# A recurrent attention kernel: the first chunk's float32 score products of a pair's two halves issued alternately

## The chip, the cores and the metric

The kernel runs on one core of one Trainium2 chip. The metric is the device time of one execution in microseconds (us). A kernel's time is the median of several runs. The profile and the trace come from one execution that was recorded by the hardware profiler.

## What is computed

The input is r, k, v, w, a, b of 4 batches x 8 heads x 768 steps x 40 elements, and the weights of two feed-forward layers. For each of the 32 heads a 40x40 state is carried over the 768 steps; then two layers work on all 3072 tokens. Cut to what matters:

```python
for t in range(S):                       # S = 768
    y[:, :, t] = einsum('bhd,bhde->bhe', r_t, state)
    Sa = einsum('bhde,bhe->bhd', state, a_t)
    state = state * w_t[:, :, None, :] - einsum('bhd,bhe->bhde', Sa, b_t)
    state = state + einsum('bhd,bhe->bhde', v_t, k_t)
x = y as 3072 tokens x 320
h = x @ w_in;  x = (h * cos(h)) @ w_out              # 320 -> 2048 -> 320
h = x @ w_in2; x = (s * relu(h)**2 + b) @ w_out2     # 320 -> 2048 -> 320
```

## The kernel before, in words

The 768 steps are cut into 12 chunks of 64 steps (`C = 64`), and the recurrence is solved chunk by chunk with matrix products. The 32 heads are 4 groups `g` of 8 (`l` counts the 8). Two groups are a pair `pg`, and they are the pair's two halves: the first lies on partitions 0 to 39, the second on partitions 64 to 103 of the same tiles.

`prep(c)` (line 1117) makes what a chunk needs of its own inputs. `load_w` brings the decays into `XX`, `scan` multiplies them up on VectorE, `stage_kb` and `stage_ar` scale k, b and a, r by them, `tz` transposes, and `sc1` (line 733) makes the first score products: for each of the 8 heads of a group one product of k and b (128 columns) with a (64 columns) over the 40 elements of a head, into one PSUM bank `s1p`. VectorE multiplies the bank with a mask and writes `M1`, and ScalarE copies the diagonal blocks of it to `ND`. When all four groups have done so, `inv_begin`, `inv`, `inv_out`, `inv_mid` and `inv_end` (lines 757 to 806) invert the triangular blocks: a transpose of `ND` to `UN`, then 30 small VectorE instructions in a row that read each other's results (`ND<-UD,UN` and `UD<-ND,UD` by turns), and products on TensorE that end in `DT`.

`chain(c, pg)` (line 1140) solves one pair of a chunk: `rhs`, `u_half`, `lmul`, `u_half` find the updates `UF` (`uhp` and `rhp` are their PSUM tiles), `sp` carries the state on, `tx` (line 902; `tx0`, line 913, in the first chunk) transposes `UF` into `XT` with a ScalarE copy behind it, `sc2` (line 924) makes the second score products of `XT` (128 columns) with r (64 columns) into a bank `s2p`, VectorE masks that into `M2`, and `yt` multiplies into the output `y`. `xs` writes y to DRAM (`x<-yhl`), and `x1_load` reads it back as the input of the first layer (`xs<-x`). `mlp` then issues the two layers in steps: `hp` is the PSUM tile of the first product and `op` that of the second; the tile `q` between them lies in a ring of 8 buffers that it shares with `XT`, `M2`, `y` and `o1`.

In chunks 1 to 11 the scores are taken from float16 parts that are stacked on 120 partitions. In the first chunk (c = 0) `sc1` and `sc2` work on float32 directly, on the 40 partitions of one half, in groups of 8 products of the same half:

```python
r = slice(g % 2 * 64, g % 2 * 64 + 40)
...
nc.tensor.matmul(ps[:, l, :], k, a, start=(l == 0), stop=True, skip_group_check=True)
```

A float32 product stands in the trace as two weight loads and two matmul records, so a group's 8 products are 16 records.

The order of the instructions on the engines isn't the order of these calls. Each call of `do` (line 1113) is a block, and every engine instruction of it is only recorded (class `Recorder`, from line 95). `schedule` (line 275) then plans all of them in one list: each instruction (for TensorE the run of products in a block) has a cost from `cost` (line 151) and a priority, which is the longest way from it to the end by these costs; whichever can start first is emitted next, and the engines run the emitted order without change. `cost` tells how long a weight load and a matmul are held to take, and it halves both where a product has at most 64 columns of weights (`side`, line 161). A block may only start when its tiles have buffers, and `caps` (line 1168) limits how many tiles of a name may be alive: `XT` 2, `M2` 2, `q` 4, and 6 of the 8 PSUM banks for all that isn't `hp` or `op` (`att`). The limit is looked at when a block starts; `tx0` takes two `XT` tiles in one block.

Since all instructions are recorded, they are emitted by line 392, and the trace has that line for nearly all of them. They are told apart by the names of their tiles.

Of the kernel before, what the change touches and what calls it, by code (L numbers as in the profile page):

```python
# [24 lines left out]
C = 64  # L25
# [69 lines left out]
class Recorder:  # L95
# [54 lines left out]
    @staticmethod  # L150
    def cost(eng, method, out, ins, k):
        size = lambda x: math.prod(c for _, c in list(x.ap)[1:])
        n = size(out)
        psum = any(x.space == PSUM for x in ins)
        if eng == "tensor":

            k, m, f = ins[0].ap[0][1], size(ins[0]), 1 + (ins[0].dtype == F32)
            if method == "transpose":
                return k * f, m * f, k / 128, k * f * f
            low = Recorder.region(out)[0] < 64  # L160
            n, side = size(ins[1]) * f * f, 2 if m <= 64 else 1
            return n if low else 0, (32 if m == 128 and f == 1 else m * f * f) / side, k / 128, n / side
        if eng == "scalar":
            return (0.05 if psum else 0.092) + n * 0.833e-3 + (0.093 if k.get("accum_out") is not None else 0) + \
                (0.093 if isinstance(k.get("bias"), bass.AP) else 0)
        if eng == "vector":
            if method == "reciprocal":
                return 0.065 + n * 6.3e-3
            if method == "tensor_tensor_scan":
                return 0.065 + n * 2.08e-3  # L170
            if method == "transpose":
                return 0.065 + n * 1.87e-3
            if method == "tensor_reduce":
                return 0.065 + size(ins[0]) * 1.04e-3
            half = method in ("tensor_scalar", "tensor_copy", "memset") and not (psum and ins[0].dtype == F32)
            return 0.065 + n * (0.52e-3 if half else 1.04e-3) + (0.063 if isinstance(k.get("scalar"), bass.AP) else 0)
        if eng == "gpsimd":
            if method in ("tensor_scalar", "memset"):
                return 0.05 + n * (1.03e-3 if method == "tensor_scalar" else 0.8e-3)
            return 0.147 + n * (2.1e-3 if out.dtype == F32 else 1.887e-3)  # L180
        b = WIDTH.get(out.dtype, 4) * math.prod(c for _, c in out.ap)
        run = min(Recorder.run(x) for x in (out, *ins) if x.ap[-1][0] == 1)
        full = max(x.ap[0][1] for x in (out, *ins) if x.space != DRAM) == 128
        return 0.45 if full else 0.625, b / (360e3 if run >= 512 else 180e3)
# [247 lines left out]
class Fast:  # L432
# [300 lines left out]
    def sc1(self, c, g):  # L733
        nc = self.nc
        ps = self.pp.tile([128, 8, C], F32, tag="at", bufs=8, name="s1p")
        for l in range(8):
            if c == 0:
                r = slice(g % 2 * 64, g % 2 * 64 + 40)
                k = self.IN["kb", c, g // 2][r, l].rearrange("p m t -> p (m t)")
                a = self.A0[g // 2, 0][r, l]  # L740
            else:
                k, a = self.KB[c, g][0:120, l, :], self.AR[c, g][0:120, l, 0:C]
            nc.tensor.matmul(ps[:, l, :], k, a, start=(l == 0), stop=True, skip_group_check=True)
        if g == 0:
            self.ND[c] = self.pst.tile([128, 16, 32], F32, tag="ND", name="ND", bufs=1)
        m = self.M1[c, g] = self.pa.tile([128, 8, C], F32, tag="M1", name="M1", bufs=7)
# [177 lines left out]
    def sc2(self, c, g):  # L924
        nc = self.nc
        ps = self.pp.tile([128, 8, C], F32, tag="at", bufs=8, name="s2p")
        for l in range(8):
            if c == 0:
                r = slice(g % 2 * 64, g % 2 * 64 + 40)
                x, ar = self.XT[0, g, l // 4][r, l % 4, :], self.A0[g // 2, 1][r, l, :]  # L930
            else:
                x, ar = self.XT[c, g][0:120, l, :], self.AR[c, g][0:120, l, C:2 * C]
            nc.tensor.matmul(ps[:, l, :], x, ar, start=(l == 0), stop=True, skip_group_check=True)
        m = self.M2[c, g] = self.pm.tile([128, 8, C], F32, tag="q", name="M2", bufs=8)
        nc.vector.tensor_tensor(out=m, in0=ps, in1=bc(self.mask2, 1, [128, 8, C]), op=ALU.mult)

# [180 lines left out]
    def prep(self, c):  # L1117
# [4 lines left out]
        for pg in range(2):  # L1122
            do(self.load_stage, c, pg)
            do(self.stage_kb, c, pg)
            do(self.load_ar, c, pg)
            do(self.stage_ar, c, pg)
            do(self.kb_out, c, 2 * pg)
            do(self.kb_out, c, 2 * pg + 1)
            for g in (2 * pg, 2 * pg + 1):
                do(self.tz, c, g)  # L1130
                do(self.sc1, c, g)
        do(self.inv_begin, c)
        do(self.inv, c)
        do(self.inv_out, c)
# [4 lines left out]

    def chain(self, c, pg):  # L1140
        g0, g1 = 2 * pg, 2 * pg + 1
        for f in [(self.rhs, c, pg), (self.u_half, c, pg, 0), (self.lmul, c, pg), (self.u_half, c, pg, 1), (self.uhl, c, g0), (self.uhl, c, g1),
                  (self.sp, c, pg), (self.tx, c, g0), (self.sc2, c, g0), (self.tx, c, g1), (self.sc2, c, g1),
                  (self.yt, c, pg), (self.ts, c, pg)]:
            self.do(*f)

# [11 lines left out]
    def run(self, es0):  # L1158
# [3 lines left out]
        with ExitStack() as es:  # L1162
# [2 lines left out]
            self.x0 = dr.tile([NC, 2, 3, 40, 768], F16, name="x0")  # L1165
            self.x1 = dr.tile([NC, 2, 128, DM], F32, name="x1")
            self.consts(pc)
            rec = self.nc = Recorder(nc, {"any": {"at", "xs", "q"}, "cls": {"XT": 2, "rhp": 3, "hp": 2, "op": 2, "xs": 2, "M2": 2, "q": 4, "att": 6}})
            rec.sink.add(self.junk.tensor.name)
            pool = lambda s, n, **k: rec.pool(s.enter_context(tc.tile_pool(name=n, bufs=1, **k)), n)  # L1170
            self.pm = pool(es, "mlp")
# [205 lines left out]
```

## Time and profile before

| what | value |
|---|---|
| median of 3 runs | 1194.1 us (1187.11, 1194.1, 1196.09) |
| the profiled execution's own time | 1188.45 us |
| its span, first to last instruction | 1186.7 us |
| TensorE matmuls busy | 1024.5 us (86%), 16094 records |
| TensorE weight loads busy | 822.7 us (69%) |
| VectorE busy | 718.7 us (61%) |
| ScalarE busy | 740.1 us (62%) |
| GpSimd busy | 437.2 us (37%) |

The rows below use the profile's short names: PE is TensorE's matmuls, PEld its weight loads, DVE is VectorE, ACT is ScalarE, POOL is GpSimd and SP is the engine that issues the DMAs (SPq is its queue). A row of the timeline is: start in us, length in us, engine, line, operation, tiles out<-in, shapes, x the number of instructions that are merged in it, and in brackets the idle time before it with what ended it. A row of the chain of waits is: start, length, engine or DMA, tiles, line and count. A row of the windows is: the stretch, its length, then for PE, PEld, DVE, ACT and POOL the busy us and the count of instructions, the granted TensorE clock, the mean busy share of the DMA engines, and GB/s.

### The profile page before, as it was taken

What the parts mean: (1) busy time and instruction counts of PE and PEld (TensorE: products, weight loads), DVE (VectorE), ACT (ScalarE), POOL (GpSimd) and SP (SyncE); (2) the same over time, 40 slices, a digit from 0 to 9 for tenths busy, and PEclk for the clock granted to TensorE, in tenths of its full rate; (3) what the DMA queues carried; (4) which work ended last, traced back from release to release, by engine and by line L of the source; (5) the groups of instructions that cost most, each with busy time, mean ns of one, the idle gap of its engine ahead of it and who ended that gap; (6) DMA issues with size and microseconds to landing.
All of it is one profiled execution on the core that took longest, in us unless ns stands there. A gap on an engine that the chain in (4) does not pass through costs nothing.

```text
span 1186.7 us, 37912 instructions
## 1 busy us (share of the span) xinstructions
PE 1024.5 (86%) x16094; PEld 822.7 (69%) x16094; DVE 718.7 (61%) x1390; ACT 740.1 (62%) x1640; POOL 437.2 (37%) x430
## 2 busy tenths in 40 slices
PE   3335878988999889989989998976999999999996
PEld 3234767776778677767777776755788888888885
DVE  6989475857573849384846553789444455454543
ACT  4466568786767677677868674766544454444443
POOL 2685455465535464536454512358300000000000
PEclk9999969999999899989998899888999999999999
DMA  9553343444433543253443222475000000000001
GB/s 229 190 193 121 114 151 116 150 126 156 138 101 122 159 144 125 95 172 109 146 137 124 86 68 73 147 185 131 27 23 23 23 23 23 23 23 23 23 13 24
DMA packets 74755, 121.15 MB, mean 102 GB/s; under 512 B 16500, under 2 KB 47348, under 8 KB 73556
## 3 DMA queue, kind: packets, MB, share of 16 engines
q1 hardware_dynamic: 74580, 118.67, 33.1%
q8 instruction: 128, 2.10, 0.8%
q14 instruction: 47, 0.39, 0.1%
HBM read 72.71 MB, written 12.29 MB: 72 GB/s over the span
## 4 chain that ended last, share of the span: by engine, by line
PE 57%; DVE 13%; DMA 12%; ACT 7%; SPq 6%; issue 4%; POOL 0%; ACTq 0%; DVEq 0%; POOLq 0%
PE hp L392 23%; PE op L392 21%; SPq L392 6%; DMA XX<-in_w 4%; PE ytp L392 3%; PE rhp L392 3%; DVE XX L392 3%; DMA wraw<-in_w 3%; DVE wraw L392 2%; DMA XT<-XT 2%; PE uhp L392 2%; DVE v L392 1%; DMA xs<-x 1%; ACT XT L392 1%; DVE w L392 1%
## 5 line engine op out<-in xcount | busy, mean ns | idle before, releaser
L392 PEld LDWEIGHTS <-w 120*128 120x128 f16 (+1 forms) x3102 | 301.1, 100 | 98.8 <-ACT w L392 33.1
L392 PE MATMUL op<-v,gh 128*128 128x320 f16 x1536 | 328.5, 304 | 3.2 <-ACT gh L392 3.0
L392 PE MATMUL op<-v,gl 128*128 128x320 f16 x768 | 232.9, 303 | 2.6 <-POOL gl L392 2.6
L392 PE MATMUL hp<-xs,w 120*128 120x256 f16 x1536 | 208.8, 287 | 11.9 <-DMA xs<-x 10.7
L392 PE MATMUL hp<-x2s,w 120*128 120x256 f16 x1536 | 189.8, 272 | 0.0
L392 POOL TENSOR_TENSOR gl<-q,gh 128x512 f16<-128x512 f32 x96 | 116.9, 1220 | 197.0 <-ACT gh L392 191.8
L392 PEld LDWEIGHTS <-gh 128*128 128x128 f16 x1536 | 144.2, 99 | 52.2 <-ACT gh L392 3.6
L392 ACT ACTIVATE q<-hp 128x512 f32<-128x512 f32 x96 | 57.2, 596 | 126.3 <-PE hp L392 126.0
L392 DVE SCALAR_TENSOR_TENSOR q<-q,s_t 128x512 f32<-128x512 f32 x96 | 72.1, 751 | 102.6 <-ACT q L392 96.8
L392 DVE SCALAR_TENSOR_TENSOR q<-hp,q 128x512 f32<-128x512 f32 x96 | 65.3, 684 | 81.0 <-ACT q L392 78.3
L392 DVE SCALAR_TENSOR_TENSOR gl<-q,b_t,gh 128x512 f16<-128x512 f32 x96 | 72.1, 752 | 48.9 <-ACT gh L392 46.8
L392 PEld LDWEIGHTS <-gl 128*128 128x128 f16 x768 | 75.8, 99 | 35.2 <-POOL gl L392 3.8
L392 ACT ACTIVATE gh<-q,b_t 128x512 f16<-128x512 f32 x96 | 69.1, 720 | 42.9 <-DVE q L392 41.8
L392 DVE TENSOR_TENSOR_SCAN XX<-XX,starts 128x264 f32<-128x264 f32 x96 | 73.1, 816 | 29.2 <-DMA XX<-in_w 28.2
L392 ACT ACTIVATE q<-hp,half_pi 128x512 f32<-128x512 f32 x96 | 65.1, 681 | 36.4 <-PE hp L392 33.7
L392 POOL TENSOR_TENSOR kb<-kb,XX 128x512 f32<-128x512 f32 x44 | 57.6, 1318 | 73.2 <-DVE XX L392 64.1
L392 ACT ACTIVATE gh<-q 128x512 f16<-128x512 f32 x96 | 59.2, 625 | 22.2 <-DVE q L392 20.2
L392 POOL TENSOR_TENSOR kbl<-kb,kbh 128x1024 f16<-128x1024 f32 x22 | 47.5, 2158 | 28.0 <-ACT kbh L392 27.5
L392 ACT ACTIVATE R<-rhp 32x320 f32<-32x320 f32 x96 | 41.1, 428 | 23.1 <-PE rhp L392 21.0
L392 PE MATMUL rhp<-UF,M 64*64 64x40 f32 (+1 forms) x1536 | 53.3, 229 | 0.8 <-ACT UF L392 0.5
L392 DVE TENSOR_TENSOR M<-s2p,mask 128x512 f32<-128x512 f32 x48 | 32.2, 685 | 34.6 <-PE s2p L392 34.5
L392 POOL TENSOR_TENSOR arl<-ar,arh 128x1024 f16<-128x1024 f32 x22 | 48.0, 2180 | 12.3 <-ACT arh L392 12.2
(184 smaller groups left out, 1787.4 us busy)
## 6 DMA issues: line engine op xcount, KB each, us to landing
XX<-in_w SPq DMA_DIRECT2D x12, 1056.0 KB
kb<-in_kb SPq DMA_DIRECT2D x24, 512.0 KB
ar<-in_ar SPq DMA_DIRECT2D x22, 512.0 KB
KB<-kbh SPq DMA_DIRECT2D x88, 80.0 KB
ars<-arh SPq DMA_DIRECT2D x88, 80.0 KB
v<-in_v SPq DMA_DIRECT2D x20, 320.0 KB
wraw<-in_w SPq DMA_DIRECT2D x8, 720.0 KB
SS<-SHL SPq DMA_DIRECT2D x88, 50.0 KB
```

The lines of the kernel that those rows point to most:

```text
L392: f(*a, **k)
```

## The change

The first chunk's score products get blocks of their own, `sc1_0` and `sc2_0`. Each makes both halves of a pair: it takes two PSUM banks, and for each of the 8 heads it issues the product of the first half and then that of the second half. What follows a group's products (mask, copies) is moved to `sc1_end` and `sc2_end` without change. In `prep`, `sc1_0` comes before the two `tz` of the pair. In `chain`, both `tx` of a pair come before `sc2_0`, which needs the four `XT` tiles of both halves; the limit on living `XT` tiles is raised from 2 to 3, for all chunks. In the planner's cost a product over at most 64 partitions is now held to take half (`k <= 64`), as one with at most 64 columns of weights is. This also touches the planned cost of the one product of `inv_begin` in each chunk, which is over one partition (tile `UD`). Chunks 1 to 11 keep `sc1` and `sc2` as they are.

```diff
--- before.py
+++ after.py
@@ -158,7 +158,7 @@
             if method == "transpose":
                 return k * f, m * f, k / 128, k * f * f
             low = Recorder.region(out)[0] < 64
-            n, side = size(ins[1]) * f * f, 2 if m <= 64 else 1
+            n, side = size(ins[1]) * f * f, 2 if m <= 64 or k <= 64 else 1
             return n if low else 0, (32 if m == 128 and f == 1 else m * f * f) / side, k / 128, n / side
         if eng == "scalar":
             return (0.05 if psum else 0.092) + n * 0.833e-3 + (0.093 if k.get("accum_out") is not None else 0) + \
@@ -734,13 +734,22 @@
         nc = self.nc
         ps = self.pp.tile([128, 8, C], F32, tag="at", bufs=8, name="s1p")
         for l in range(8):
-            if c == 0:
-                r = slice(g % 2 * 64, g % 2 * 64 + 40)
-                k = self.IN["kb", c, g // 2][r, l].rearrange("p m t -> p (m t)")
-                a = self.A0[g // 2, 0][r, l]
-            else:
-                k, a = self.KB[c, g][0:120, l, :], self.AR[c, g][0:120, l, 0:C]
+            k, a = self.KB[c, g][0:120, l, :], self.AR[c, g][0:120, l, 0:C]
             nc.tensor.matmul(ps[:, l, :], k, a, start=(l == 0), stop=True, skip_group_check=True)
+        self.sc1_end(c, g, ps)
+
+    def sc1_0(self, pg):
+        ps = [self.pp.tile([128, 8, C], F32, tag="at", bufs=8, name="s1p") for _ in range(2)]
+        for l in range(8):
+            for hf in range(2):
+                r = slice(hf * 64, hf * 64 + 40)
+                k = self.IN["kb", 0, pg][r, l].rearrange("p m t -> p (m t)")
+                self.nc.tensor.matmul(ps[hf][:, l, :], k, self.A0[pg, 0][r, l], start=(l == 0), stop=True, skip_group_check=True)
+        for hf in range(2):
+            self.sc1_end(0, 2 * pg + hf, ps[hf])
+
+    def sc1_end(self, c, g, ps):
+        nc = self.nc
         if g == 0:
             self.ND[c] = self.pst.tile([128, 16, 32], F32, tag="ND", name="ND", bufs=1)
         m = self.M1[c, g] = self.pa.tile([128, 8, C], F32, tag="M1", name="M1", bufs=7)
@@ -925,12 +934,21 @@
         nc = self.nc
         ps = self.pp.tile([128, 8, C], F32, tag="at", bufs=8, name="s2p")
         for l in range(8):
-            if c == 0:
-                r = slice(g % 2 * 64, g % 2 * 64 + 40)
-                x, ar = self.XT[0, g, l // 4][r, l % 4, :], self.A0[g // 2, 1][r, l, :]
-            else:
-                x, ar = self.XT[c, g][0:120, l, :], self.AR[c, g][0:120, l, C:2 * C]
-            nc.tensor.matmul(ps[:, l, :], x, ar, start=(l == 0), stop=True, skip_group_check=True)
+            nc.tensor.matmul(ps[:, l, :], self.XT[c, g][0:120, l, :], self.AR[c, g][0:120, l, C:2 * C], start=(l == 0), stop=True, skip_group_check=True)
+        self.sc2_end(c, g, ps)
+
+    def sc2_0(self, pg):
+        ps = [self.pp.tile([128, 8, C], F32, tag="at", bufs=8, name="s2p") for _ in range(2)]
+        for l in range(8):
+            for hf in range(2):
+                r = slice(hf * 64, hf * 64 + 40)
+                self.nc.tensor.matmul(ps[hf][:, l, :], self.XT[0, 2 * pg + hf, l // 4][r, l % 4, :], self.A0[pg, 1][r, l, :],
+                                      start=(l == 0), stop=True, skip_group_check=True)
+        for hf in range(2):
+            self.sc2_end(0, 2 * pg + hf, ps[hf])
+
+    def sc2_end(self, c, g, ps):
+        nc = self.nc
         m = self.M2[c, g] = self.pm.tile([128, 8, C], F32, tag="q", name="M2", bufs=8)
         nc.vector.tensor_tensor(out=m, in0=ps, in1=bc(self.mask2, 1, [128, 8, C]), op=ALU.mult)
@@ -1126,9 +1144,12 @@
             do(self.stage_ar, c, pg)
             do(self.kb_out, c, 2 * pg)
             do(self.kb_out, c, 2 * pg + 1)
+            if c == 0:
+                do(self.sc1_0, pg)
             for g in (2 * pg, 2 * pg + 1):
                 do(self.tz, c, g)
-                do(self.sc1, c, g)
+                if c:
+                    do(self.sc1, c, g)
         do(self.inv_begin, c)
         do(self.inv, c)
         do(self.inv_out, c)
@@ -1139,8 +1160,9 @@
     def chain(self, c, pg):
         g0, g1 = 2 * pg, 2 * pg + 1
+        sc2 = [(self.tx, c, g0), (self.tx, c, g1), (self.sc2_0, pg)] if c == 0 else [(self.tx, c, g0), (self.sc2, c, g0), (self.tx, c, g1), (self.sc2, c, g1)]
         for f in [(self.rhs, c, pg), (self.u_half, c, pg, 0), (self.lmul, c, pg), (self.u_half, c, pg, 1), (self.uhl, c, g0), (self.uhl, c, g1),
-                  (self.sp, c, pg), (self.tx, c, g0), (self.sc2, c, g0), (self.tx, c, g1), (self.sc2, c, g1),
+                  (self.sp, c, pg), *sc2,
                   (self.yt, c, pg), (self.ts, c, pg)]:
             self.do(*f)
@@ -1165,7 +1187,7 @@
             self.x0 = dr.tile([NC, 2, 3, 40, 768], F16, name="x0")
             self.x1 = dr.tile([NC, 2, 128, DM], F32, name="x1")
             self.consts(pc)
-            rec = self.nc = Recorder(nc, {"any": {"at", "xs", "q"}, "cls": {"XT": 2, "rhp": 3, "hp": 2, "op": 2, "xs": 2, "M2": 2, "q": 4, "att": 6}})
+            rec = self.nc = Recorder(nc, {"any": {"at", "xs", "q"}, "cls": {"XT": 3, "rhp": 3, "hp": 2, "op": 2, "xs": 2, "M2": 2, "q": 4, "att": 6}})
             rec.sink.add(self.junk.tensor.name)
             pool = lambda s, n, **k: rec.pool(s.enter_context(tc.tile_pool(name=n, bufs=1, **k)), n)
             self.pm = pool(es, "mlp")
```

## Rows read from the trace of the kernel before

**Rows 1.** Windows: five stretches of the whole run, all engines.

```profile
20.00:125.00 105.00, 52.35 (x801) 45.93 (x802) 89.25 (x190) 63.52 (x165) 68.82 (x76) 1.00 0.57 172
125.00:175.00 50.00, 37.15 (x752) 31.95 (x747) 29.96 (x63) 33.49 (x86) 23.63 (x31) 0.83 0.44 137
175.00:850.00 675.00, 605.58 (x11774) 478.34 (x11772) 427.34 (x875) 481.17 (x1072) 339.96 (x290) 0.94 0.40 124
850.00:1186.70 336.70, 327.45 (x2770) 265.08 (x2768) 161.06 (x241) 156.93 (x306) 0.00 (x0) 0.99 0.09 24
```

**Rows 2.** The chain of waits that ended last, from 110 us on.

```profile
117.53 3.60 PE s2p L392 x16
...
156.40 8.28 DMA XX<-in_w
```

**Rows 3.** Timeline of TensorE, 18 to 36 us.

```profile
19.66 3.68 PE L392 MATMUL s1p<-ars,kb 40*128 40x64 f32 x16
...
24.39 8.91 PE L392 MATMUL s1p<-ars,kb 40*128 40x64 f32 x48
```

**Rows 4.** Windows: the instructions of tile s1p alone, two short stretches.

```profile
27.10:27.70 0.60, 0.60 (x8) 0.60 (x8) 0.00 (x0) 1.00 1.15 235
28.00:29.00 1.00, 1.00 (x8) 1.00 (x6) 0.69 (x1) 1.00 1.14 249
```

**Rows 5.** Timeline of VectorE: mask, scans, the first and the last inverse instruction.

```profile
37.81 0.68 DVE L392 TENSOR_TENSOR M<-s1p,mask 128x512 f32<-128x512 f32 x1
...
42.02 7.10 DVE L392 TENSOR_TENSOR_SCAN XX<-XX,starts 128x264 f32<-128x264 f32 x8 [0.30 <-DMA XX<-in_w]
...
50.21 0.16 DVE L392 TENSOR_TENSOR ND<-UD,UN 128x15 f32<-128x15 f32 x1
...
71.05 0.18 DVE L392 SCALAR_TENSOR_TENSOR UD<-ND,UD 128x15 f32<-128x15 f32 x1
```

**Rows 6.** Timeline of TensorE, 85 to 175 us.

```profile
85.62 1.27 PE L392 MATMUL uhp<-R,DT 32*32 32x40 f32 x30 [1.61 <-DVE M L392]
...
93.69 1.90 PE L392 MATMUL txp<-ident_f,UF 128*40 128x128 f32 x8 [0.52 <-ACT UF L392]
...
117.45 3.67 PE L392 MATMUL s2p<-ars,XT 40*128 40x64 f32 x16
...
127.56 1.89 PE L392 MATMUL txp<-ident_f,UF 128*40 128x128 f32 x8
...
144.33 3.67 PE L392 MATMUL s2p<-ars,XT 40*128 40x64 f32 x16 [2.23 <-ACT XT L392]
...
151.42 1.93 PE L392 MATMUL ytp<-M,Z 128*40 128x64 f32 x32
...
174.64 4.49 PE L392 MATMUL hp<-xs,w 120*128 120x256 f16 x24
```

**Rows 7.** Timeline of ScalarE: the copies of the second halves.

```profile
117.63 0.59 ACT L392 ACTIVATE XT<-txp 40x512 f32<-40x512 f32 x1
...
143.69 1.07 ACT L392 ACTIVATE XT<-txp 40x512 f32<-40x512 f32 x2
```

**Rows 8.** Timeline of GpSimd and SP: y on its way to the first layer.

```profile
156.80 1.24 POOL L392 TENSOR_TENSOR yhl<-y,yhl 128x512 f16<-128x512 f32 x1
...
164.75 0.71 SPq L392 DMA_DIRECT2D x<-yhl  x2
```

**Rows 9.** One tile: XT in chunks 1 to 11, 175 to 775 us.

```profile
L392 ACT ACTIVATE XT<-txp x44: 996/1011/1021, 180.9 to 768.3; 80x1024 f16<-80x1024 f16 x44
...
  DMA XT<-XT: 14.6, 12
```

**Rows 10.** Timeline of all engines: two XT tiles of a later chunk.

```profile
278.64 1.58 SPq L392 DMA_DIRECT2D XT<-XT  x2
...
283.12 0.41 PE L392 MATMUL s2p<-ars,XT 120*128 120x64 f16 x8 [2.82 <-DMA XT<-XT]
```

**Rows 11.** One tile: UD, the product of inv_begin.

```profile
L392 PE MATMUL UD<-eyes,row x12: 371/385/604, 5.7 to 682.9; 1*128 1x512 f16 x12
```

## The prediction

> **What bounds the kernel now.** I read the windows by stage first, then the chain of waits, then the timelines of single engines. The windows [rows 1] show three different limits. From 175 us on TensorE is the bound: 605.58 of 675 us busy, then 327.45 of 336.7. Between 20 and 125 us it is busy for only 52.35 of 105 us while VectorE has 89.25, and between 125 and 175 for 37.15 of 50. So the start leaves TensorE 65.5 us without work, and the stage after it has 69.4 us idle in 675. The change takes work from TensorE only in the first chunk, where it has time to spare. It can help only if it brings the first chunk's y forward, and with it the first product of the first layer, which starts at 174.64 [rows 6] and fills TensorE from there on.
>
> The chain of waits [rows 2] names a score product once in this stage, 3.60 us of `s2p` at 117.53; the other pieces there are weight conversions on VectorE and DMAs such as the 8.28 us for the decays at 156.40. So most of the start isn't TensorE's, and I look at what stands before and behind the two kinds of score products.
>
> **What two halves cost side by side.** A half's 16 records take 3.68 us when alone, and 48 records in a row, three halves, take 8.91 [rows 3], where three times 3.68 would be 11.04. The difference is at the places where one half follows the other. Around such a place 8 records are in flight within 0.60 us; away from it 8 in 1.00 us [rows 4]. The weights of the second half are already loading while the first half still multiplies. Thus two halves that alternate should run next to each other all the way. From above the price of a pair is 2 x 3.68 = 7.36 us, from below 3.68, one half's time. I take 3.74, a half's time and one short step, because the rows at the handover are of exactly this form.
>
> The Trainium skill has a measurement that is less kind: its page "TensorE: Matmul & The Clock Gate", section "Measured speedup vs the span model" of Part 3, gives 3.07 times for four row tiles. Worked out for two tiles in proportion that would be about 1.5 times, an estimate from that page, or 4.8 us for a pair in place of 3.74. The forecast would lose under 2 us by it.
>
> **Part A, the first products.** Before, the four halves end at 24.39 + 8.91 = 33.30 us. After, the first pair ends at 19.66 + 3.74 = 23.40; the same pause to 24.39 follows (norms of weights), and the second pair ends at 28.13: 5.2 us earlier, or 2 us later if nothing runs side by side (19.66 + 4 x 3.68 + 1.0 = 35.4). What comes of it goes through VectorE. The last mask is read at 37.81, 4.5 us after its product [rows 5], because weight conversions stand ahead of it. Then 7.10 us of scans for the second chunk run from 42.02, and the first of the 30 inverse instructions starts only at 50.21, the last ends at 71.23: 21.0 us, 0.70 each, with conversions between them. With products 5.2 us earlier the transposition could come before the scans, and some of the 30 could run before 42.02. The copy and the transposition now lie between the mask and the scans; so if all of it moves with the products, the inverse could start at 42.02 - 5.2 = 36.8, and the gain from above is 50.21 - 36.8 = 13.4 us. From below it is nothing, if VectorE's order keeps the scans first. But `uhp`, the next product of the chain, starts at 85.62, 14 us after the inverse, and it was a bank that VectorE had to free that ended its wait [rows 6]. VectorE's own work isn't reduced and has only 15.75 us of room in 105 [rows 1]. I take -2 us, near the lower end.
>
> **Part B, the second products.** Now the second half of a pair waits in the order for the first: transposes at 93.69 and 127.56, last product ending at 117.45 + 3.67 = 121.12 and 144.33 + 3.67 = 148.00 [rows 6], so 27.4 and 20.4 us for the two pairs. The copies of the second halves end at 117.63 + 0.59 and 143.69 + 1.07 = 144.76 [rows 7]. After the change both halves' transposes stand together: 2 x 1.89 us. If ScalarE copies all four tiles as they come, the last copy ends some 8 us after the first transpose, and 3.74 us of products follow: 11.7 us in place of 20.4, a gain of 8.7 us for the second pair, which ends the chunk. If ScalarE's order leaves the copies where they are, behind conversions that wait for weights, the products end at 144.76 + 3.74 = 148.5, 0.5 us later than now. I take -5 us for `ytp` at 151.42 [rows 6], a bit over half, since the transposes can move but the copies still share ScalarE with conversions. The waiting added to the first half's product costs nothing more: `yt` needs both halves anyway, and what stands behind it on TensorE is the next `uhp`, whose first pair it doesn't delay by more than the 3.67 us that the second product no longer takes.
>
> **From y to the first layer.** GpSimd finishes y's low part at 156.80 + 1.24 = 158.04, and its write is issued at 164.75 [rows 8]: 6.7 us in which SP issues other things, the next chunk's decays among them. That cover could eat what A and B bring. I let all 7 us pass, because the planner places the write anew with the rest.
>
> **The other edits.** The new planned cost of `inv_begin` changes nothing on the chip: the product takes 385 ns [rows 11] as before, and only its place in the order may move. The limit of 3 on `XT` is at work in all chunks. It lets a transposition start earlier, but `XT` tiles are not on the state's path from chunk to chunk; their cost is bounded under the rivals, and I take 0.
>
> **The sum.** A -2 and B -5 give -7 us at the first layer, and since TensorE is busy 90% of the time from there, I carry them to the end one to one: 1188.45 - 7 = 1181.5 for the profiled execution. The median of the runs, 1194.1, is 5.65 above that execution, so on its scale 1187.1. One per cent, about what a measurement of this kernel can tell from no change, is 11.9 us.
>
> **The rivals.** *Hidden anyway.* VectorE, SP and the weights set the start, and y comes when it came: 1194. For it speak the chain, with one score product in this stage [rows 2], and the mask read 4.5 us after its product [rows 5]; against it the 20.4 us of which only 3.67 are the last product. The Trainium skill warns of this on the page "TensorEngine Tiling (Array Packing)", section "PSUM Bottleneck": tiling speeds TensorE up, not the emptying of PSUM. For the first products that late mask agrees.
>
> *Everything carried.* The inverse moves ahead of the scans (13.4 us) and the second pair gains its full 8.7: 22.1 us, 1194.1 - 22.1 = 1172.0. For it speaks TensorE's idle 65.5 us in the start; against it that VectorE has hardly any room there.
>
> *Slower: three `XT` tiles starve the ring.* At the limits before, `XT` 2, `M2` 2 and `q` 4 fill the 8 buffers; with 3 the layer's `q` finds one less. A later chunk's `XT` is alive long: its copy takes 1.01 us [rows 9], its DMAs are issued at 278.64 and its product ends at 283.53 [rows 10], so about 6 us with the copy. Idle time now is 69.4 us for 11 chunks, 6.3 each [rows 1]; if the missing buffer adds a quarter, 1.5 us a chunk, the time is 1194.1 + 16.5 = 1210.6. It decides from the point where more than 4 `q` and `XT` tiles wait at once in most chunks. Against it: POOL and ACT free a `q` within a few us.
>
> *Not side by side.* Then a pair's first bank comes 3.68 us later, in both kinds of product: 1194.1 + 7.4 = 1201.5. Against it stand the handovers [rows 4].
>
> **How the numbers follow.** Forecast 0.42 (1180 to 1193), hidden 0.20, everything carried 0.22, starved ring 0.13, not side by side 0.03. Faster by over 1%, below 1182.2: most of the carried case (0.20) and the low end of the forecast (0.13), 0.33. Slower by over 1%, above 1206: 0.10 of the ring and 0.05 for a worse order after the first chunk, taken from hidden, 0.15. The rest is 0.52. The range: 1171 takes in the carried case, 1206 leaves out most of the ring.
>
> **What would show it.** Right: `s1p` 32 records in under 4.2 us, `s2p` likewise; the first inverse instruction before 50.21; `ytp` of the second pair near 146 and the first `hp` near 168. Wrong: the first `hp` still at 174 or later, or TensorE's idle time from 175 to 850 us far from 69 us, which would mean that the order of the later chunks and not the first one made the difference.

## The result, and the profile after

The changed kernel takes 1178.1 us (median of 4 runs, 1174.8 to 1180.4) where the kernel before takes 1195.1 beside it (4 runs, 1187.1 to 1197.0): the ratio is 0.9864, with a 95% interval of 0.982 to 0.9909. That is 1.4% faster, by more than the 1% that a measurement of this kernel can tell, and inside the predicted range. A ratio leaves out the runs that lie over 1.5% above the fastest of their kernel and a median counts all of them, so the two can differ: of one kernel below, at 1202.0 us, five of the eleven runs are left out. The profiled execution took 1180.35 us, with a span of 1178.6, against 1188.45 and 1186.7 before: 8.1 us less. The medians are 17 us apart; the profiled execution lies at the upper end of the changed kernel's runs and near the lower end of the other's. The traces are read below for their 8.1 us, and times are told by medians.

The windows by stage, as in [rows 1]; the columns are the stretch, then busy us and count of TensorE, of its weight loads, VectorE, ScalarE and GpSimd, and last the granted clock, the DMA share and GB/s:

```profile
20.00:125.00 105.00, 47.60 (x908) 41.11 (x909) 87.17 (x190) 67.49 (x175) 70.14 (x78) 0.88 0.59 168
125.00:175.00 50.00, 33.78 (x680) 28.04 (x680) 32.63 (x66) 27.65 (x69) 18.14 (x23) 0.56 0.47 143
175.00:850.00 675.00, 607.73 (x11795) 479.46 (x11794) 434.79 (x876) 486.29 (x1092) 342.44 (x296) 0.94 0.40 125
850.00:1178.60 328.60, 319.62 (x2707) 258.99 (x2705) 157.32 (x236) 152.55 (x296) 0.00 (x0) 0.99 0.09 22
```

TensorE has less work before 175 us (81.38 against 89.50) and is busy for 607.73 of 675 us after it, 2 us more than before. The clock recorded as granted in the start fell, from 1.00 and 0.83 to 0.88 and 0.56; how far that can be believed comes up at the end.

The timeline of TensorE, to set beside [rows 3, 6] (start, duration, what, and the idle time before it with what ended it):

```profile
19.95 3.68 PE L392 MATMUL s1p<-ars,kb 40*128 40x64 f32 x32
...
26.82 3.68 PE L392 MATMUL s1p<-ars,kb 40*128 40x64 f32 x32
...
82.85 1.28 PE L392 MATMUL uhp<-R,DT 32*32 32x40 f32 x32 [1.70 <-ACT DT L392]
...
104.03 3.68 PE L392 MATMUL s2p<-ars,XT 40*128 40x64 f32 x32
...
124.89 3.32 PE L392 MATMUL txp<-ident_f,UF 128*40 128x128 f32 x16
...
131.74 2.39 PE L392 MATMUL s2p<-ars,XT 40*128 40x64 f32 x18
138.90 1.97 PE L392 MATMUL s2p<-ars,XT 40*128 40x64 f32 x14 [4.77 <-ACT XT L392]
...
143.46 1.94 PE L392 MATMUL ytp<-M,Z 128*40 128x64 f32 x32
...
170.04 3.81 PE L392 MATMUL hp<-xs,w 120*128 120x256 f16 x24
```

Two halves, 32 records, take 3.68 us in both kinds of product, exactly the 3.68 of one half's 16 records alone [rows 3]. The second pair's `s2p` doesn't run in one piece: after 18 records TensorE waits 4.77 us for ScalarE's copy of the last `XT`. `uhp` ends 2.8 us earlier, the second pair's transposes start 2.7 earlier, its `ytp` 8.0 and the first layer's first product 4.6.

The timeline of VectorE, for [rows 5] and for the second pair's y:

```profile
32.47 1.27 DVE L392 TENSOR_TENSOR M<-s1p,mask 128x512 f32<-128x512 f32 x2
...
36.89 0.16 DVE L392 TENSOR_TENSOR ND<-UD,UN 128x15 f32<-128x15 f32 x1
...
43.03 6.48 DVE L392 TENSOR_TENSOR_SCAN XX<-XX,starts 128x264 f32<-128x264 f32 x8
...
71.22 0.17 DVE L392 SCALAR_TENSOR_TENSOR UD<-ND,UD 128x15 f32<-128x15 f32 x1
...
150.59 0.33 DVE L392 TENSOR_SCALAR vraw<-vraw 128x320 int32<-128x320 int32 x1 [7.59 <-DMA vraw<-in_v]
...
150.83 0.68 DVE L392 SCALAR_TENSOR_TENSOR y<-ytp,XX 128x512 f32<-128x512 f32 x1
```

The inverse now begins at 36.89, before the scans, 13.3 us earlier than in [rows 5], and its last instruction ends at 71.39, 0.16 later than before. And y, whose product was ready by 145.4, is made only at 150.83: VectorE sat idle for 7.59 us behind a weight conversion that waits for its DMA and stands ahead of y in its order. SP's rows tell why that DMA is late: it is issued behind six transfers of the state, `SS`.

```profile
141.69 4.63 SPq L392 DMA_DIRECT2D SS<-SHL  x6
...
147.28 1.62 SPq L392 DMA_DIRECT2D vraw<-in_v  x2
```

In the kernel before the same line reads

```profile
153.40 0.69 DVE L392 SCALAR_TENSOR_TENSOR y<-ytp,XX 128x512 f32<-128x512 f32 x1 [2.31 <-PE ytp L392]
```

where y waited for its product. So 8.0 us at the product became 2.6 at y. SP's timeline has the rest of the way:

```profile
155.86 0.84 SPq L392 DMA_DIRECT2D x<-yhl  x2
156.79 1.65 SPq L392 DMA_DIRECT2D KB<-kbh  x2
...
163.49 0.43 SPq L392 DMA_DIRECT2D xs<-x  x1
```

The write of y is issued 8.9 us earlier than in [rows 8], since less stands ahead of it, but the next chunk's `KB` transfers now come between it and the read `xs`. The read gains 6.3 us (it was issued at 169.76), and the first layer's product, behind work of the next chunk on TensorE, 4.6.

The lead doesn't stay what it is. Taking the first `hp` of each later chunk in both traces, the changed kernel is 3.0 us ahead at chunk 1, 9.9 behind at chunk 2, 17.9 ahead at chunk 4, 3.3 behind at chunk 8 and 8.1 ahead at chunk 11. So the 8 us of the end are not simply the 4.6 of the start carried along. The windows from the first layer's first product to VectorE's last y, and from there to the end, tell where they lie, the first fence of before, the second of after:

```profile
174.64:777.15 602.51, 547.57 (x11361) 435.52 (x11360) 368.82 (x815) 436.37 (x963) 289.55 (x224) 0.95 0.39 125
777.15:1186.70 409.55, 385.81 (x3184) 308.17 (x3183) 219.95 (x305) 201.74 (x414) 50.41 (x67) 0.97 0.16 41
```

```profile
170.04:767.49 597.45, 551.34 (x11375) 436.90 (x11373) 378.77 (x819) 437.40 (x972) 294.05 (x231) 0.95 0.39 125
767.49:1178.60 411.11, 380.98 (x3172) 305.70 (x3170) 218.30 (x307) 202.78 (x418) 51.13 (x68) 0.97 0.17 42
```

The start is 4.6 us shorter, the stretch up to the last y 5.1 shorter and the end 1.6 longer. In the middle stretch TensorE sits idle for 46.1 us instead of 54.9 and is busy 3.8 us longer. The end begins with the loads of the second layer's weights, which are issued when attention is done; VectorE's last y and SP's issue, before:

```profile
777.15 0.69 DVE L392 SCALAR_TENSOR_TENSOR y<-ytp,XX 128x512 f32<-128x512 f32 x1 [0.16 <-PE ytp L392]
783.90 3.63 SPq L392 DMA_DIRECT2D wraw<-in_w  x4
```

and after:

```profile
767.49 0.68 DVE L392 SCALAR_TENSOR_TENSOR y<-ytp,XX 128x512 f32<-128x512 f32 x1
775.35 3.63 SPq L392 DMA_DIRECT2D wraw<-in_w  x4
```

What made the time shorter here lies ahead of the last y, which comes 9.7 us earlier.

### The profile page after: what moved, and what is told of

It reads as the page before. It is cut to its first block, busy times and chain, and to the rows that moved or that the text cites. A ratio compares the mean times of both kernels' runs of the same rounds, so it can differ in the third digit from the quotient of the medians.

```text
span 1178.6 us, 37909 instructions
## 1 busy us (share of the span) xinstructions
PE 1010.4 (86%) x16094; PEld 808.7 (69%) x16094; DVE 722.7 (61%) x1390; ACT 738.7 (63%) x1640; POOL 435.6 (37%) x430
## 4 chain that ended last, share of the span: by engine, by line
PE 54%; DVE 13%; DMA 10%; ACT 9%; issue 5%; POOL 4%; SPq 4%; ACTq 0%; DVEq 0%; POOLq 0%
PE hp L392 22%; PE op L392 20%; SPq L392 4%; DVE XX L392 3%; PE rhp L392 2%; DMA wraw<-in_w 2%; DVE v L392 2%; PE ytp L392 2%; PE uhp L392 2%; DMA ars<-arl 2%; DMA XX<-in_w 1%; DMA v<-in_v 1%; ACT q L392 1%; DVE wraw L392 1%; ACT junk L392 1%
## 5 line engine op out<-in xcount | busy, mean ns | idle before, releaser
L392 ACT ACTIVATE ND<-M 32x256 f32<-32x256 f32 x96 | 39.6, 413 | 24.7 <-DVE M L392 23.4
```

The lines of the kernel that those rows point to most:

```text
L392: f(*a, **k)
```

## The experiments

Two things are mixed in the change. The products are faster on the chip, and the planner, which orders every engine's instructions by planned costs, gets another list of operations and writes another order for the whole kernel. The experiments take them apart. Ratios are against the kernel before, run beside each. The changed kernel once more ran beside the three experiments that follow it below; the later ones are compared with it through these ratios.

**The changed kernel once more**, as the measure for the rest.

> The changed kernel once more, beside the kernel before and the three others of this call on one chip, so that they can be compared. Every theory expects the ratio again, 0.982 to 0.991 of the kernel before, 1174 to 1181 us.

Median 1175.5 us of 10 runs, 1191.1 for the kernel before: 0.988 [0.9842, 0.9919]. With the first measurement, the gain is 1.2 to 1.4%.

**The same order, halves one after the other.** In both new functions the two loops change places, so that every engine's order is that of the changed kernel, and only the array's rows are no longer used side by side:

```diff
-        for l in range(8):
-            for hf in range(2):
+        for hf in range(2):
+            for l in range(8):
```

> The changed kernel with the same blocks, costs and order on every engine; only inside the two new blocks all 8 products of the first half come first and then those of the second. Theory 1, the gain is that the two halves run side by side on the chip: the s1p and s2p blocks take about 6.5 to 7.4 us instead of 3.68, the second s2p block ends some 3 us later, and the time rises by 4 to 8 us over the changed kernel. Theory 2, the gain is the new order of the instructions: the blocks take as long as in theory 1, but the time stays within 3 us of the changed kernel, and well below the kernel before.

Median 1176.7 us of 6 runs, 0.9886 [0.9833, 0.9939]: no difference from the changed kernel that can be seen. The intervals reach half a per cent, some 6 us, to either side, so the time alone doesn't exclude the low end of theory 1's 4 to 8 us. Yet the products are slower, as TensorE's timeline shows:

```profile
19.66 6.29 PE L392 MATMUL s1p<-ars,kb 40*128 40x64 f32 x32
...
104.64 6.29 PE L392 MATMUL s2p<-ars,XT 40*128 40x64 f32 x32
...
132.77 6.29 PE L392 MATMUL s2p<-ars,XT 40*128 40x64 f32 x32
...
141.65 1.94 PE L392 MATMUL ytp<-M,Z 128*40 128x64 f32 x32
...
166.21 3.98 PE L392 MATMUL hp<-xs,w 120*128 120x256 f16 x24
```

A pair takes 6.29 us instead of 3.68, and still the first layer starts no later than in the changed kernel (166.21 against 170.04, 169.0 in its second profile). With the trace, which shows no delay behind them, the parallel products as such are worth nothing that can be measured; the order is.

**The limit of 3 on `XT` alone**, on the kernel before (`"XT": 2` becomes `"XT": 3`).

> The kernel before with one edit: the limit on living XT tiles is 3 instead of 2, so that the second half's transposes of the first chunk can start before the first half's products are done. Theory 1, side by side: no gain, 1190 to 1198 us. Theory 2a, the order gains because both transposes come before the products: most of the gain, 1178 to 1186 us, and the first hp some 4 us earlier than 174.6. Theory 2b, the gain is one throw of a plan that is sensitive to any edit: a change of up to 12 us to either side.

Median 1186.3 us of 12 runs, 0.9971 [0.9939, 1.0002]: within 1%. It falls between theory 1's and theory 2a's times, and 2b allows it. Its first `hp` starts at 169.0, 5.7 us ahead of before, as 2a wanted, but its last y is only 1.9 ahead, and the profiled execution, the slowest of the twelve, ends 6.2 us later than before's. Here too a lead at the start isn't one at the end.

**The planned cost alone**, on the kernel before (`2 if m <= 64 or k <= 64 else 1`).

> The kernel before with one edit: the planned cost of a product over at most 64 partitions is halved, while nothing on the chip is done differently. Theories 1 and 2a: no gain, 1190 to 1198 us. Theory 2b, the plan is sensitive to any edit: it moves by 5 to 12 us to one side or the other, with the difference made in late chunks.

Median 1184.1 us of 12 runs, 0.9941 [0.9906, 0.9976]. An edit that changes no instruction, only the planned costs and with them the order, brings 0.6%, as theory 2b alone expected. No run takes the planned cost, or the limit of 3 in the later chunks, out of the changed kernel, so how much of its gain hangs on either stays open.

**The first products alone, and the second alone.** From the changed kernel, the first takes back the limit of 2, `sc2` and the order of `chain`, of which the last is shown:

```diff
-        sc2 = [(self.tx, c, g0), (self.tx, c, g1), (self.sc2_0, pg)] if c == 0 else [(self.tx, c, g0), (self.sc2, c, g0), (self.tx, c, g1), (self.sc2, c, g1)]
+        sc2 = [(self.tx, c, g0), (self.sc2, c, g0), (self.tx, c, g1), (self.sc2, c, g1)]
```

> The change's first half alone: the first score products as a block of both halves, the second ones as before (limit on XT 2). Theory 1, from the prediction: a small part of the gain, 2 of 7 us, so 1186 to 1193 us. Theory 2b, one throw of a sensitive plan: anywhere from 1172 to 1200 us, and not a share of the change's gain that adds up with the other half's; the time follows the last y of chunk 11, some 415 us before the end.

The other takes back `sc1` and keeps the rest, the limit of 3 with it:

```diff
-            if c == 0:
-                do(self.sc1_0, pg)
...
-                if c:
-                    do(self.sc1, c, g)
+                do(self.sc1, c, g)
```

> The change's second half alone: the second score products as a block of both halves with both transposes before it (limit on XT 3), the first ones as before. Theory 1, from the prediction: most of the gain, 1180 to 1187 us, with the first hp about 5 us before 174.6. Theory 2b: anywhere from 1172 to 1200 us, whatever the first hp does; the time follows the last y of chunk 11, some 415 us before the end.

The first products alone: 1183.0 us (11 runs), 0.9929 [0.9904, 0.9953]. The second alone: 1180.2 us (5 runs), 0.9887 [0.9833, 0.994]. Their sum would be 1.8% and the whole is 1.2 to 1.4%. With the first alone, the first layer starts at 176.7, later than before (174.64), and the kernel is faster all the same. So its gain can't come from an earlier start, and its time lies outside the prediction's 1186 to 1193. The second alone lands on both signs of the prediction, 1180 to 1187 us and a first `hp` (169.1) about 5 us earlier, so it doesn't tell the theories apart. From the last y to the end both take 405 us, not the 415 that was expected.

**More work in the first chunk, the same order.** Each `sc2_0` block is issued three times; the planner counts it once, so the order stays (the flag `extra` makes the recorder keep a call without planning it; its lines in `Recorder` are not shown):

```diff
-        for l in range(8):
-            for hf in range(2):
+        for e in range(3):
+            self.nc.extra = e > 0
+            for l in range(8):
+                for hf in range(2):
```

> The changed kernel in the same order on every engine, with extra time on TensorE in the first chunk: each second score product block is issued three times over, with the same result, so 7.4 us more for each of the two pairs, 14.7 in all. Step of the prediction, what comes at the first layer's start is carried to the end one to one: first hp 7 to 15 us later and the time 7 to 15 us up, 1183 to 1191 us. Theory 3, the chunks after it absorb it because the pace of the later chunks and the end of the last one set the time: the last y and the time move by less than 4 us.

Median 1182.8 us of 11 runs, 0.9906 [0.9873, 0.9939]; the interval overlaps that of the changed kernel for the most part. The median is 7.3 us above the changed kernel's 1175.5, by the ratios it is 3 us, so the time alone decides little. TensorE:

```profile
104.17 10.51 PE L392 MATMUL s2p<-ars,XT 40*128 40x64 f32 x96
...
148.36 1.94 PE L392 MATMUL ytp<-M,Z 128*40 128x64 f32 x32
...
168.20 3.19 PE L392 MATMUL hp<-xs,w 120*128 120x256 f16 x24
```

and VectorE:

```profile
148.54 0.33 DVE L392 TENSOR_SCALAR vraw<-vraw 128x320 int32<-128x320 int32 x1 [1.73 <-DMA vraw<-in_v]
...
150.34 0.69 DVE L392 SCALAR_TENSOR_TENSOR y<-ytp,XX 128x512 f32<-128x512 f32 x1 [1.47 <-PE ytp L392]
```

`ytp` comes 4.9 us later than in the changed kernel, y 0.5 earlier and the first layer 1.8 earlier. Three executions whose first chunk is that of the changed kernel (its two profiles and that of the last experiment with added work below) have their `ytp` at 143.46, 141.61 and 138.47, y at 150.83, 150.18 and 146.08 and the first layer at 170.04, 168.99 and 166.24, so these places vary by 4 to 5 us anyway. `ytp` is later here than in any of them, y and the first layer aren't. The wait of the weight conversion shrank from 7.59 to 1.73 us: the later product is swallowed by it.

**The last product of the first chunk seven times**, the sharper test of the same cover, by the same flag in `yt` for chunk 0, pair 1 (`for e in range(7 if (c, pg) == (0, 1) else 1)`).

> The changed kernel in its order, with extra time on TensorE at the y of the first chunk's second pair: its products (ytp) are issued seven times over, the last time counts and the result is the same; 6 x 2.47 = 14.8 us before that y, on the way to the first hp at 169 to 170. If the place has cover as the second score products had (14.7 us there moved nothing), the first hp and the time stay. If not, the first hp comes 7 to 15 us later, and then: the prediction's step, one to one from there to the end, expects the last y and the time later by as much; theory 3, the later chunks absorb it, expects the last y and the time within 4 us.

Median 1180.3 us of 8 runs, 0.9928 [0.9891, 0.9965]. The size of the delay was missed: the repeats took less than the first did.

```profile
139.17 1.94 PE L392 MATMUL ytp<-M,Z 128*40 128x64 f32 x32
...
148.51 1.09 PE L392 MATMUL ytp<-M,Z 128*40 128x64 f32 x32
...
168.02 3.43 PE L392 MATMUL hp<-xs,w 120*128 120x256 f16 x24
```

The last `ytp` starts 9.3 us after the first. VectorE's timeline:

```profile
147.29 0.33 DVE L392 TENSOR_SCALAR vraw<-vraw 128x320 int32<-128x320 int32 x1 [8.31 <-DMA vraw<-in_v]
...
149.66 0.69 DVE L392 SCALAR_TENSOR_TENSOR y<-ytp,XX 128x512 f32<-128x512 f32 x1 [2.04 <-PE ytp L392]
```

Of the 9.3 us some 7.3 pass while VectorE waits for the weight anyway, and 2.04 show as y's own wait. y is still 1.2 us earlier than in the changed kernel, since the weight came earlier in this execution, and the first layer starts at 168.0. The time is some 0.5% above the changed kernel's, with intervals that overlap, and the last y of this execution, at 765.5, is where the changed kernel's is (765.1 in its second profile); so whether the half per cent is real stays open. As in the run before, no delay reached the first layer, so what would become of one that did, in this order, neither run tests.

**More work in the last chunk, the same order.** The `sc2` products of chunk 11 are issued 16 times, some 14 us, to see whether a delay there carries.

```diff
-        for l in range(8):
+        for e in range(16 if c == NC - 1 else 1):
+            nc.extra = e > 0
+            for l in range(8):
```

> The counterpart of the run before: about the same extra time on TensorE in the last chunk. The changed kernel in the same order, with each of the four second score product groups of chunk 11 issued 16 times over, same result; at about 0.24 us each that is 3.6 us a group, 14 in all. One to one and theory 3 both expect the last y 7 to 14 us later and the time 7 to 14 us up, 1183 to 1190 us; if the time stays, the last y doesn't set it and theory 3 falls.

Median 1183.8 us of 11 runs, 0.9945 [0.9912, 0.9977], 0.65% or some 8 us above the changed kernel, with intervals that barely overlap. In the trace VectorE's last y and SP's issue of the weight loads read

```profile
778.86 0.69 DVE L392 SCALAR_TENSOR_TENSOR y<-ytp,XX 128x512 f32<-128x512 f32 x1
786.01 3.63 SPq L392 DMA_DIRECT2D wraw<-in_w  x4
```

13.8 and 12.9 us later than in the changed kernel's second profile (765.1 and 773.1), and the span is 14.8 longer (1189.0 against 1174.2). So in one and the same order a delay that reaches the last y is carried to the end in the trace. That execution lies 6.9 us above its kernel's median, so the median shows some 8 of the 14 us. Beside it the early delay's median, 1182.8, is only 1.1 us lower (0.9906 and 0.9945, with intervals that overlap): it is the traces that tell the two apart, by where the delay ends, and not the times.

**Three other orders for the same work.** One planned latency of TensorE is moved by a thousandth of a microsecond, which changes nothing but the planner's choices: 0.28 to 0.281 on the kernel before and on the changed one, and another, 0.14 to 0.141, on the changed one.

```diff
-            op.lat = 0.28
+            op.lat = 0.281
```

> The kernel before with the planned latency of a TensorE instruction at 0.281 us instead of 0.28: nothing is done differently on the chip, only the plan falls out differently. Theory 2b, part of the change's gain is one throw of the plan: a ratio other than 1 to the kernel before, between 0.985 and 1.01. If the plan isn't sensitive, 0.997 to 1.003.

> The changed kernel with the same edit, planned latency of a TensorE instruction 0.281 instead of 0.28. If the change's gain holds for any plan, the ratio to the kernel before stays 0.984 to 0.992. Theory 2b: it differs from that, between 0.98 and 1.0, and the mean over the plans with and without the change differs by less than the 1.2 to 1.4 per cent of this one pair.

> The changed kernel with the planned latency of a VectorE, ScalarE or GpSimd instruction at 0.141 us instead of 0.14. As for the run before: 0.984 to 0.992 if the gain holds for any plan, otherwise between 0.98 and 1.0.

Before with 0.281: 1202.0 us, 1.0029 [0.998, 1.0078]. Changed with 0.281: 1185.1 us, 0.9942 [0.9906, 0.9977]. Changed with 0.141: 1189.3 us, 0.9975 [0.9938, 1.0013] (11 runs each). On the kernel before, the ratio falls into the 0.997 to 1.003 of a plan that isn't sensitive, though the median of all eleven runs is 0.9% above that of before (1191.3); that one is not settled. On the changed kernel, a thousandth of a microsecond in a planned latency takes away half of the gain of the change, with intervals that overlap a little, or four fifths, with intervals that don't.

All plans together: without parallel products or the order made for them, 1 (before), 0.9941, 0.9971 and 1.0029, mean 0.9985; with the whole change, 0.988, 0.9942 and 0.9975, mean 0.9932; with half of it, 0.9929 and 0.9887. The means differ by 0.5%, some 6 us, but the two groups overlap (0.9941 without, 0.9975 with), so that four plans and three don't show how much the change brings for whatever plan comes.

## Why the prediction was right, and where it wasn't

**The price of a pair**, 3.74 us, was right: 3.68 in the three pairs that run in one piece; the second pair's `s2p` waits in between for a copy. The reading behind it, that the records at the handover from one half to the other show how two halves run that alternate [rows 4], holds over the whole block. The estimate of 1.5 times, 4.8 us, was too cautious here. It was worked out in proportion from the Trainium skill's page "TensorE: Matmul & The Clock Gate", section "Measured speedup vs the span model" of Part 3, whose 3.07 is for four row tiles. Two halves in one half's time are a factor of 2 on 2 x 3.68 us, and 1.7 on the 6.29 us that two halves take one after the other. The rival that they wouldn't run side by side is out.

**Part A**, -2 us: `uhp` ended 2.8 us earlier and the second pair's transposes 2.7, so the size was right. The way wasn't. The inverse started at 36.89, almost the 36.8 of the upper bound, and ended no earlier (71.39 against 71.23), since the scans and more of VectorE's conversions now lie between its instructions: 13.3 us of lead at its start are gone at its end. The 2.8 us arise later: `ydp` still starts at 72.53 (72.37 before), and `uhp` behind it now waits for `DT` and no longer for VectorE's `M`.

**Part B**, -5 us: from the second pair's transposes to `ytp` it took 151.42 - 127.56 = 23.9 us before and 143.46 - 124.89 = 18.6 after, 5.3 less. The doubt that the copies share ScalarE with conversions was right too: 4.77 of the 18.6 us are the wait for the last copy, and in the other executions of this order without added work there the stretch takes 13.7 to 16.4 us, so the size depends on the execution. Both terms together are 8.0 us at `ytp`, where 7 were forecast.

**"I let all 7 us pass"** was the first step that failed. The prediction named SP's 6.7 us as a possible cover and let it go, and indeed the write of y was issued 8.9 us earlier. The cover lay one engine earlier, on VectorE, where no term of the sum looked: the conversion of a weight that waits 7.59 us for its DMA stands ahead of y. 8.0 us became 2.6 at y, and 4.6 at the first layer after SP and TensorE had placed other work. That this is cover and not chance is shown by the two kernels that delay `ytp` in the same order and start the first layer no later (168.2 and 168.0, where the undelayed order starts it at 166.2 to 170.0), and by the serial halves (166.2). In the executions in which y isn't delayed on purpose it follows SP's first `SS` transfer by 9.0 to 9.2 us, whenever `ytp` is ready. In the words of the rivals, for the speed of the products it was *hidden anyway*.

**"I carry them to the end one to one"** was the second, and the larger. The argument was that TensorE is busy for 90% of the time from the first layer on. But the later chunks are ordered anew too, and a lead at the first layer says nothing about the end under another order: with the limit of 3 alone 5.7 us of lead became 1.9 at the last y; with the first products alone a start 2.1 us later went with a span 7.5 shorter. From the first `hp` to the end of the span, the five traces of the changed kernel's order without added work in the last chunk take 1005 to 1009 us, although the first `hp` lies anywhere from 166.2 to 170.0; the eight other orders, the one before among them (1012), take 1002 to 1024. So the step may hold within one order, where it wasn't tested, and fails from one order to the next. The delay in chunk 11 shows that the time of the last y is carried, and that within one order: under the other orders the rest of the span took 404 to 418 us. All four signs that the prediction named for being right appeared (3.68 us for a pair in one piece, the inverse at 36.89, `ytp` even at 143.46, the first `hp` at 170.04), and its condition for being wrong, TensorE's idle time from 175 to 850 us far from 69 us, did not, with 67.3 us. They couldn't tell this case: the stretch has fixed ends, and up to the last y 8.8 us of idle time went out while behind it, where TensorE has less left to do until the second layer starts, 6.4 came in.

**The starved ring** didn't show: TensorE's idle time up to the last y didn't rise, and the limit of 3 alone gives 0.9971. *Everything carried* gives 1172.0, within a few microseconds of the measured medians (1175.5 and 1178.1), but by a mechanism that isn't there: the inverse's 13.4 us were not carried.

So the number was inside the range and the account of it half right. The forecast itself was 7 us, 1187.1 as a median; measured are 15.6 and 17.0 us, over twice that and outside the 1180 to 1193 of its own case, and it is the room left for *everything carried* that took them in. That the profiled execution, at 1180.35, lies 1 us from the 1181.5 forecast for it is luck: 4.6 us of its gain are there at the first layer and 3.5 came from the order behind it, which the sum put at nothing. The terms in the first chunk came out about as worked, and a good part of the time they were meant to save, 8.0 us at `ytp` and 4.6 at the first layer, was swallowed on the way. That the kernel is 1.2 to 1.4% faster is, as far as intervals of half a per cent can tell, a property of the order of instructions that the planner wrote for it: the same order with serial halves has all of it, and a thousandth of a microsecond in a planned latency moved the changed kernel's ratio by 0.6 and 1%. What stays open is how much of it the change would bring under any plan, and by which steps in the later chunks an order becomes better.

## What to carry to other kernels

Where a planner writes the order, an edit is two edits, the work and the order: keep the order and undo the work (swap two loops, repeat a product outside the plan) before you credit the work with the gain, and measure a few orders that differ by a meaningless planned number to see how far the order alone moves the time. A product that comes earlier helps only if what consumes it is next in its engine's order; look at what stands ahead of it there, and at what that waits for. And don't carry a lead from one order into another; here the only point from which a delay was seen to reach the end, within one order, is the last step before a stage that can't start earlier, the last y.

## What the runs showed of the hardware

Two halves of these float32 products over 40 rows that alternate take 3.68 us in the first chunk, as long as one half alone; one after the other they take 6.29.

In the changed kernel a pair of first products runs where the profile shows a granted clock of 1.00 and a pair of second ones where it shows 0.50 (the levels of 2.4 and 1.2 GHz), and both take 3.68 us. It looks as if the clock didn't matter to them, but it does. The second profile of the changed kernel has 16 records of a second product inside a short stretch at 1.00. The windows of these products alone, first there, then a second and a first product of the first profile:

```profile
131.90:132.80 0.90, 0.89 (x16) 0.89 (x17) 0.00 (x0) 1.00 0.99 342
```

```profile
104.00:104.90 0.90, 0.87 (x8) 0.87 (x10) 0.00 (x0) 0.50 0.23 77
```

```profile
19.95:20.85 0.90, 0.90 (x8) 0.90 (x10) 0.00 (x0) 1.00 1.03 241
```

In 0.90 us there are 16 records at 1.00 and 8 at 0.50, and one record takes 272 ns (the median) or 417. The first product, with 8 records of 418 ns, runs as at 0.50 although 1.00 is shown. So the 1.00 that the profile shows in the start isn't what the products had. Other rows say the same. Every `ytp` begins with one float16 product of 512 columns. Three of them in the kernel before, and the windows around these:

```profile
122.26 0.61 PE L392 MATMUL ytp<-ident,zeros 128*128 128x512 f16 x1
...
190.28 0.39 PE L392 MATMUL ytp<-ident,zeros 128*128 128x512 f16 x1
...
257.74 0.63 PE L392 MATMUL ytp<-ident,zeros 128*128 128x512 f16 x1
```

```profile
122.20:122.90 0.70, 0.70 (x7) 0.20 (x5) 0.00 (x0) 0.51 (x2) 0.70 (x3) 1.00 0.32 111
190.20:190.70 0.50, 0.50 (x11) 0.23 (x9) 0.50 (x1) 0.50 (x2) 0.00 (x0) 1.00 0.81 180
257.70:258.40 0.70, 0.70 (x5) 0.10 (x4) 0.00 (x0) 0.42 (x1) 0.70 (x1) 0.50 0.31 103
```

At a shown 1.00 the product takes 0.39 us at 190 us and 0.61 at 122, and 0.63 where 0.50 is shown. The rest of `ytp` goes with it: 1.94 us at 122.80, 1.09 at 190.60, 1.91 at 258.30. In the first chunk the product takes 0.58 to 0.61 us in all fourteen traces (the first time, where it is repeated), whatever clock they show there.

So the fall to 0.57 from 100 to 125 us, where the kernel before shows 1.00, isn't one that the products felt: the 512 columns take 0.61 us at 111.53 after and at 122.26 before. And the repeats of `ytp` took 1.09 us where the first took 1.94 because the clock rose: it is shown as 0.50 at the first and 1.00 at the last, and the products of 512 columns beside them take 0.61 and 0.39.
